# Attention followed by routed experts: blocks behind five groups of the first batch instead of six

## The chip, the cores and the metric

The kernel runs on one core of a Trainium2 chip. The metric is the device time of one execution in microseconds, as the median of several runs. The core's engines are TensorE (matmuls), VectorE, ScalarE, GpSimd (here mostly scatters with indices) and SyncE, which only issues DMAs. Each engine works through its own instructions in the order in which they stand; semaphores make it wait for other engines and for DMAs.

## The reference

Four batches of q, k and v, each 5056 x 256 in float32. Attention is over channels: columns of q and k are normalised over the 5056 tokens, s is a 256 x 256 matrix, and each token's v is multiplied with its softmax. The result goes through a layer of eight experts, of which each token uses the one with the largest logit.

```python
qn = q / (np.linalg.norm(q, axis=1, keepdims=True) + 1e-06)
kn = k / (np.linalg.norm(k, axis=1, keepdims=True) + 1e-06)
s = kn.transpose(0, 2, 1) @ qn / tau
a = softmax(s)                      # over the last axis, 256 x 256
x = (v @ a).reshape(20224, 256)
expert_idx = np.argmax(x @ w_gate, axis=1)
# for each expert e, on its tokens:
h = np.maximum(xe @ w1[e], 0.0)     # 256 -> 1024
out[mask] = gate_w[mask, None] * (h @ w2[e])
```

## The kernel before

For each batch, `attention` first reads q and k in 20 chunks of 256 tokens (`raw`, line 205, 512 KB each). ScalarE squares a chunk (line 217), VectorE adds the squares up (line 218), and TensorE multiplies k with q into two accumulators `sp` (line 225). In the second batch and later a chunk can be split into a high and a low half (`hl`, line 188 on ScalarE, line 189 on VectorE; products in lines 229 and 230). Norms and softmax follow (lines 242 to 303). Then ten groups of 512 tokens each are made into rows of x: TensorE multiplies v with the softmax (`px`, line 365), ScalarE copies the result out and squares it (`xg`, lines 370 and 372), ScalarE and VectorE write two float16 halves of each row (`rows`, lines 386 and 387), VectorE finds the expert, TensorE ranks the tokens of a group within their experts (`rtp`, lines 423 and 426), and GpSimd scatters the rows by expert into `xs` in DRAM, four scatters a group (line 445). The last of the small steps ahead of a group's scatters are the reciprocal in line 433 and the slot numbers in line 442.

`weights` prepares the eight experts' matrices, 16 in all, each loaded in two halves (`W` and `wraw`, line 120). TensorE sums up squares (`gram`, lines 158 and 123), which sets a scale; then ScalarE and VectorE each run once over the matrix to make two float16 halves (lines 112 and 113). It is a generator: each step that is taken from it issues one load.

`table` (lines 500 to 573) turns the counts of the tokens that are scattered so far into a list of full blocks of 256 tokens: `c_tb`, an expert and a place in `xs` for each block (its last step is line 571). `block_load` has SyncE read an entry (line 581), load the block's tokens transposed (`xT`, line 586) and their factors (`mt`, line 588). `block` copies the expert's weights to `wp` (VectorE, line 604), multiplies in two layers (`hp`, line 616, and `y`, line 638), and GpSimd scatters the result to `out` (line 653). There are 72 full blocks and 18 smaller ones. Before a stage's blocks can be loaded, all rows of that stage must be scattered. Stage 0 is made of the first `CUT` groups of the first batch; stage 1 of the whole first batch, and so on.

What is put in which order: the work of the first batch (`first`), the loads of the weights (`wts`) and the first chunks of the second batch (`second`) are interleaved by the loop in line 707, one half of a group of x in each step; a scheduler then orders each engine's instructions. Blocks start behind that loop, and from there the rest of the second batch and all later batches run between the pieces of blocks, paced by the two lists `marks` and `amounts`. `START` makes up for the chunks that were taken already. Buffers set waits too: a chunk of q and k from the second batch on, and a group of v from group `CUT` on, share three buffers (`raw`); `mt` has three, freed by the output scatters of a block.

Of the kernel before, what the change touches and what calls it, by code (L numbers as in the profile page):

```python
# [23 lines left out]
E, F = 8, 1024  # L24
# [3 lines left out]
BLK = 256  # L28
G = 10
T = 4  # L30
CUT = 6

SORTED = [CUT * T * P] + [N * (b + 1) for b in range(B)]
SURE = [-(-(n - E * (BLK - 1)) // BLK) for n in SORTED]
# [29 lines left out]
def attention_then_experts(ctx, tc, qk, vT, wts_in, kc, out):  # L64
# [127 lines left out]
    def attention(b, s_split, x_split, acc):  # L192
# [139 lines left out]
        def v_load(g):  # L332

            if g < CUT and g not in v_ahead:
                v_ahead[g] = [
                    work.tile([P, 512], F32, tag=tag, name=f"v{c}", bufs=bufs)
                    for c, (tag, bufs) in enumerate((("wp", WP), ("ht", 4)))
                ]
                for c in range(2):
                    sync.dma_start(out=v_ahead[g][c], in_=vT[b, g, :, c, :])  # L340

        for g in range(G):
            if b == 0 and g < CUT:
                v_load(g)
# [98 lines left out]
            for t in range(T):  # L443
# [4 lines left out]
                )  # L448
                scattered(0 if b == 0 and g < CUT else b + 1, ins)
            yield 200  # L450
# [6 lines left out]
    def scattered(stage, ins):  # L457
        raw = ins.ins
        for s2 in range(LAST):
            tc.declare_no_dep(raw, group=f"scatter{s2}", reason="slots differ")  # L460
        tc.declare_no_dep(raw, group="loads", reason="blocks read are full already")
        tc.declare_no_dep(raw, group="pads", reason="behind the tokens")
        tc.add_to_no_dep_group(f"scatter{stage}", raw)
        written[stage].append(raw.name)
# [200 lines left out]
    def take(gen, n):  # L665
        for _ in range(n):
            next(gen, None)
        return n

    nch = NP // P // 2  # L670
    normal = [(ps_a, "acc")] * 2
    wts = weights()
# [33 lines left out]
    weighed = 0  # L706
    for step in range(2, nch + 1 + 2 * CUT):
        take(first, 1)
        weighed += take(wts, 0 if step < nch else min(14 if step == nch else 2, 4 * E + 1 - weighed))
        if step > nch + 2:  # L710
            take(second, 1)
    tables = {0: table(0)}
# [13 lines left out]
    ATT = nch * 2 * 640 + 5000 + G * GRP  # L726
    START = -(2 * CUT - 2) * 2 * 640
    marks = [0.0] + [SURE[b] - EARLY for b in range(1, B)]
# [69 lines left out]
```

## Time and profile before

| | |
|---|---|
| median of 3 runs | 1184.86 us (1183.29 to 1185.75) |
| profiled execution | 1188.32 us, span 1186.6 us |
| TensorE busy | 1153.5 us, 97% of the span |
| VectorE busy | 899.4 us, 76% |
| ScalarE busy | 643.5 us, 54% |
| GpSimd busy | 392.3 us, 33% |
| mean granted clock of TensorE | 0.991 |

The time of an execution is a little longer than the span, which runs from the first to the last instruction that the profile shows. The shares are means over the whole span; the first 200 us, where weights are prepared and the first batch is worked through, differ from the rest, where blocks and attention run side by side.

### The profile page before, as it was taken

The numbers are of one execution on the slowest core, as the hardware profiler recorded it, in microseconds if no ns is written. First come the engines' busy times: TensorE is split into PE (matmuls) and PEld (weight loads), VectorE is DVE, ScalarE is ACT, GpSimd is POOL, SyncE is SP. The second block draws the span as 40 slices with busy tenths as digits, with TensorE's granted clock in tenths as the row PEclk, the third lists the DMA queues.
The fourth block names the chain that finished last, engine by engine and source line by source line (L and its number), as shares of the span: only waits on it lengthen the run. The fifth ranks groups of instructions, "written<-read, shape, count | busy, mean of one in ns | idle before, by whom it ended". The sixth has DMA issues, their size and how long they took to land.

```text
span 1186.6 us, 28182 instructions
## 1 busy us (share of the span) xinstructions
PE 1153.5 (97%) x10242; PEld 1024.9 (86%) x10242; DVE 899.4 (76%) x2384; ACT 643.5 (54%) x1362; POOL 392.3 (33%) x366
## 2 busy tenths in 40 slices
PE   9798899999999999999999999999999999999998
PEld 8677688899888889999888889999988888889897
DVE  6789988778887877777888777776875566656886
ACT  6399854877655536665565536666533223332232
POOL 0046761466511123544422212455421111112121
PEclk9989989999999999999999999999999999999999
DMA  9977765445555524444354434443242222111121
GB/s 340 408 277 254 208 177 134 135 122 145 139 145 120 130 81 101 118 115 119 97 152 127 131 91 93 131 95 82 70 109 50 50 55 55 46 51 38 40 52 35
DMA packets 147871, 145.93 MB, mean 123 GB/s; under 512 B 115980, under 2 KB 117393, under 8 KB 147728
## 3 DMA queue, kind: packets, MB, share of 16 engines
q1 hardware_dynamic: 132336, 102.48, 33.0%
q0 software_dynamic: 15392, 41.60, 9.8%
q8 instruction: 82, 1.34, 0.5%
q14 instruction: 61, 0.50, 0.1%
HBM read 80.03 MB, written 43.29 MB: 104 GB/s over the span
## 4 chain that ended last, share of the span: by engine, by line
PE 57%; issue 24%; DVE 7%; POOL 5%; ACT 3%; DMA 3%; SPq 1%; POOLq 0%; DVEq 0%; ACTq 0%
PE y L638 20%; PE hp L616 19%; PE px L368 7%; POOL out L653 4%; PE sp L225 4%; PE sp L229 3%; DMA raw<-in_qk 2%; PE sp L230 2%; DVE W L113 1%; ACT xjunk L372 1%; PE px L365 1%; DVE rows L387 1%; DVE hl L189 1%; ACT W L112 1%; ACT xg L370 1%
## 5 line engine op out<-in xcount | busy, mean ns | idle before, releaser
L616 PE MATMUL hp<-xT,wp 128*128 128x256 f16 (+1 forms) x4320 | 450.0, 262 | 1.6 <-DVE ht L624 1.1
L638 PE MATMUL y<-wp,ht 128*128 128x256 f16 x3888 | 447.7, 273 | 0.0
L616 PEld LDWEIGHTS <-wp 128*128 128x128 f16 x4320 | 383.1, 98 | 46.1 <-issue 3.4
L638 PEld LDWEIGHTS <-ht 128*128 128x128 f16 x3888 | 373.9, 98 | 53.3 <-issue 4.7
L653 POOL DMA_INDIRECT out<-o,mt x162 | 184.9, 1141 | 628.5 <-ACT o L651 595.2
L604 DVE COPY wp<-W 128x1024 f16 x720 | 297.8, 425 | 116.0 <-PE y L638 65.3
L623 ACT ACTIVATE ht<-hp 128x512 f16<-128x512 f32 x324 | 191.6, 593 | 157.1 <-PE hp L616 143.1
L624 DVE SCALAR_TENSOR_TENSOR ht<-hp,ht 128x512 f16<-128x512 f32 x324 | 219.6, 686 | 22.6 <-ACT ht L623 16.6
L445 POOL DMA_INDIRECT xs<-rows,r_si x160 | 189.5, 1184 | 122.7 <-issue 41.8
L651 ACT ACTIVATE o<-y,b_fac 128x256 f32<-128x256 f32 x162 | 68.8, 470 | 207.2 <-PE y L638 196.6
L368 PE MATMUL px<-a_h,hl 128*128 128x264 f32 x480 | 98.1, 296 | 0.0
L386 ACT ACTIVATE rows<-xg,x_sc 128x256 f16<-128x256 f32 x160 | 69.9, 497 | 25.7 <-DVE r_ex L419 16.0
L368 PEld LDWEIGHTS px<-a_h,hl 128*128 128x128 f32 x480 | 78.8, 188 | 1.6 <-issue 0.6
L189 DVE TENSOR_TENSOR hl<-raw,hl 128x1024 fp32r<-128x1024 f32 x47 | 57.4, 1221 | 26.7 <-ACT hl L188 26.7
L188 ACT CAST hl<-raw 128x1024 fp32r<-128x1024 f32 x47 | 49.1, 1044 | 45.2 <-PE sp L230 38.2
L229 PE MATMUL sp<-hl 128*128 128x512 f32 x188 | 72.3, 418 | 1.1 <-DVE hl L189 1.1
L225 PE MATMUL sp<-raw 128*128 128x256 f32 x264 | 65.3, 403 | 7.5 <-DMA raw<-in_qk 7.5
L387 DVE SCALAR_TENSOR_TENSOR rows<-xg,x_sc,rows 128x256 f16<-128x256 f32 x160 | 69.5, 477 | 1.2 <-ACT rows L386 0.8
L217 ACT ACTIVATE raw<-raw 128x1024 f32<-128x1024 f32 x44 | 46.6, 1058 | 42.6 <-DVE hl L189 42.4
L372 ACT ACTIVATE xjunk<-xg 128x256 bf16<-128x256 f32 x160 | 66.7, 417 | 3.2
L368 PE MATMUL px<-a_l,hl 128*128 128x264 f32 x240 | 68.2, 284 | 0.0
L225 PEld LDWEIGHTS sp<-raw 128*128 128x128 f32 x264 | 52.0, 202 | 15.9 <-DMA raw<-in_qk 8.6
(144 smaller groups left out, 926.4 us busy)
## 6 DMA issues: line engine op xcount, KB each, us to landing
raw<-in_qk SPq DMA_DIRECT2D x80, 512.0 KB, 4.2
vraw<-in_vT SPq DMA_DIRECT2D x34, 512.0 KB, 5.1
W<-in_w SPq DMA_DIRECT2D x28, 512.0 KB, 8.5
v<-in_vT SPq DMA_DIRECT2D x12, 256.0 KB
out<-o,mt POOLq DMA_INDIRECT x162, 2.4
xs<-rows,r_si POOLq DMA_INDIRECT x160, 4.0
wraw<-in_w SPq DMA_DIRECT2D x4, 512.0 KB, 6.5
xT<-xs SPq DMA_TRANSPOSE x90, 3.9
```

The source lines that it names most:

```text
L225: pe.matmul(sp[c][:, 0, :], raw[:, j, kc0 : kc0 + P], raw[:, j, 0:C], start=first, stop=last)
L229: pe.matmul(sp[c], hl[:, 0, j, kc0 : kc0 + P], hl[:, :, j, 0:C], start=first, stop=False)
L368: pe.matmul(px, hl[:, vh, c, ts], ah[:, c, :], start=(n == 0), stop=(n == 5))
L372: act.activation(junk, xg[:, t, 0:C], AF.Square, accum_out=ss[:, t : t + 1])
L387: vec.scalar_tensor_tensor(out=r16[:, t, C : 2 * C], in0=x, scalar=sc[:, t : t + 1], in1=r16[:, t, 0:C], op0=ALU.mult, op1=ALU.subtract,)
L445: ins = pool.indirect_dma_start(out=xs[:, :], out_offset=bass.IndirectOffsetOnAxis(ap=si[:n, t : t + 1], axis=0), in_=rows[:n, t, :], in_o ...
L604: copied[0] = vec.tensor_copy(out=t, in_=Wf[:, ds(e * 8192 + n * 1024, 1024)]).ins
L616: pe.matmul(hp[:, f % nf, :], wp[:, dc, wh, (f % 2) * P : (f % 2 + 1) * P], xT[:, 2 * xh + dc, :], start=(n == 0), stop=(n == 5),)
L623: act.activation(ht[:, 0], hp, AF.Relu)
L624: vec.scalar_tensor_tensor(out=ht[:, 1], in0=hp, scalar=0.0, in1=ht[:, 0], op0=ALU.max, op1=ALU.subtract)
L638: pe.matmul(ys[j], hts[f // nf][:, hh, f % nf, j * P : (j + 1) * P], wp[:, f % 2, wh, :], start=(f == 0 and n == 0), stop=(f == 7 and n == 2),
L653: pool.indirect_dma_start(out=out[:, :], out_offset=bass.IndirectOffsetOnAxis(ap=mt.bitcast(I32)[:, j, 1:2], axis=0), in_=o, in_offset=Non ...
```

## The change

`CUT` goes from 6 to 5. Stage 0 has then three blocks instead of five, and stage 1 nine instead of seven; the loop that precedes the blocks has two steps less, so that two chunks fewer of the second batch are taken in it. The loop takes 10 weight loads at its start instead of 14, which puts the first group of x in front of the third expert's weights, then 2 in each of two steps, and 3 instead of 2 in each later step.

```diff
-CUT = 6
+CUT = 5
...
     for step in range(2, nch + 1 + 2 * CUT):
         take(first, 1)
-        weighed += take(wts, 0 if step < nch else min(14 if step == nch else 2, 4 * E + 1 - weighed))
+        weighed += take(wts, 0 if step < nch else min(10 if step == nch else 2 if step < nch + 3 else 3, 4 * E + 1 - weighed))
         if step > nch + 2:
             take(second, 1)
```

On SyncE's queue, behind the 20 chunks of the first batch, loads of weights (`W`) and of v for the first groups stood like this before:

```order
L120 DMA W<-in_w 128x1024 x14
L340 DMA v_518<-in_vT 128x512
L340 DMA v_519<-in_vT 128x512
L340 DMA v_522<-in_vT 128x512
L340 DMA v_523<-in_vT 128x512
L120 DMA W<-in_w 128x1024 x4
L340 DMA v_644<-in_vT 128x512
L340 DMA v_645<-in_vT 128x512
L120 DMA W<-in_w 128x1024 x2
L205 DMA raw<-in_qk 128x1024
```

and stand like this now (other numbers, the same tiles):

```order
L120 DMA W<-in_w 128x1024 x10
L340 DMA v_468<-in_vT 128x512
L340 DMA v_469<-in_vT 128x512
L340 DMA v_472<-in_vT 128x512
L340 DMA v_473<-in_vT 128x512
L120 DMA W<-in_w 128x1024 x4
L340 DMA v_594<-in_vT 128x512
L340 DMA v_595<-in_vT 128x512
L120 DMA W<-in_w 128x1024 x3
L205 DMA raw<-in_qk 128x1024
```

The v of the first two groups moved ahead of four loads of weights, and a third weight load came in front of the second batch's first chunk.

Further on in SyncE's queue, from the third block's load on (`c_tb` is a table entry, `xT` and `mt` are the block's loads, `raw` the second batch's chunks), before:

```order
L581 TENSOR_LOAD c_tb
L586 ISA
L586 DMA_TRANSPOSE xT<-xs 128x4x256
L588 ISA
L588 DMA mt<-xs 128x2x2
L205 DMA raw<-in_qk 128x1024 x4
L581 TENSOR_LOAD c_tb
L586 ISA
L586 DMA_TRANSPOSE xT<-xs 128x4x256
L205 DMA raw<-in_qk 128x1024 x3
L588 ISA
L588 DMA mt<-xs 128x2x2
```

and now, from the load of v for the tenth group on:

```order
L349 DMA vraw<-in_vT 128x1024
L581 TENSOR_LOAD c_tb
L586 ISA
L586 DMA_TRANSPOSE xT<-xs 128x4x256
L588 ISA
L588 DMA mt<-xs 128x2x2
L205 DMA raw<-in_qk 128x1024 x7
L581 TENSOR_LOAD c_tb
L586 ISA
L586 DMA_TRANSPOSE xT<-xs 128x4x256
L588 ISA
L588 DMA mt<-xs 128x2x2
```

The tenth group's v now stands between the second and the third block's load; seven chunks (8 to 14) stand between the third and the fourth block's load, where four (11 to 14) stood, and the three chunks that stood between the fourth block's `xT` and `mt` are behind both.

On TensorE, where the first block begins (`px` is a group of x, `rtp` a rank, `sp_714` and `sp_715` or `sp_673` and `sp_674` the second batch's products, `hp` the block's first layer), before:

```order
L426 MATMUL rtp<-r_ex,ones_80 128x8
L365 MATMUL px<-a_x,vraw 128x264 x5
L616 LDWEIGHTS wp
L616 MATMUL hp<-xT,wp 128x256
```

```order
L426 MATMUL rtp<-r_ex,ones_80 128x8
L365 MATMUL px<-a_x,vraw 128x264 x2
L225 MATMUL sp_673<-raw 128x256
L225 MATMUL sp_674<-raw 128x256
L365 MATMUL px<-a_x,vraw 128x264 x2
L616 LDWEIGHTS wp
L616 MATMUL hp<-xT,wp 128x256
```

In the second piece, which is the order now, half of chunk 8 stands in front of the first block; before, 11 chunks were loaded ahead of the blocks' loads, and the first block began before the next was needed.

## Rows read from the trace of the kernel before

**Rows 1.** The page: the granted clock in 40 equal slices, in tenths.

```profile
PEclk9989989999999999999999999999999999999999
```

**Rows 2.** Windows: start:end, length, busy us of each engine, granted clock, DMA share.

```profile
58.50:62.50 4.00, 4.00 (x11) 3.14 (x12) 3.14 (x4) 3.50 (x4) 0.00 (x0) 0.52 1.03 407
...
80.00:100.00 20.00, 19.75 (x140) 16.77 (x139) 18.24 (x45) 18.49 (x41) 14.48 (x10) 0.93 0.76 260
...
100.00:120.00 20.00, 14.15 (x93) 11.59 (x91) 19.39 (x52) 19.56 (x41) 14.68 (x11) 1.00 0.70 236
...
148.40:153.00 4.60, 4.56 (x13) 3.36 (x14) 2.06 (x9) 2.66 (x4) 3.47 (x5) 0.50 0.71 276
```

**Rows 3.** Timeline of TensorE: start, us, line, count, idle before and its releaser.

```profile
58.04 0.59 PE L123 MATMUL gram<-w_dsum,ones 128*128 128x2 f32 x2 [4.88 <-DVE w_diag L162]
...
58.49 5.70 PE L365 MATMUL px<-a_x,v 128*128 128x264 f32 x16
...
125.04 6.03 PE L365 MATMUL px<-a_x,vraw 128*128 128x264 f32 x26
...
148.44 3.78 PE L225 MATMUL sp<-raw 128*128 128x256 f32 x8 [2.88 <-DMA raw<-in_qk]
...
186.13 1.47 PE L616 MATMUL hp<-xT,wp 128*128 128x256 f16 x12 [1.06 <-DVE ht L624]
```

**Rows 4.** Chain of waits, 120 to 170 us: start, us, what.

```profile
130.68 5.07 DMA xs<-rows,r_si
...
135.90 1.34 SPq L586
...
143.04 5.36 DMA raw<-in_qk
...
152.22 2.49 PE hp L616 x12
...
156.16 1.73 PE sp L225 x8
...
163.55 1.31 PE hp L616 x12
```

**Rows 5.** Timeline of GpSimd, scatters and outputs; columns as in rows 3.

```profile
106.24 1.29 POOL L445 DMA_INDIRECT xs<-rows,r_si  x1 [3.08 <-DVE scales L85]
...
107.84 2.95 POOL L445 DMA_INDIRECT xs<-rows,r_si  x1 [0.30 <-ACT W L112]
...
121.06 3.80 POOL L445 DMA_INDIRECT xs<-rows,r_si  x1 [0.30 <-issue]
...
130.68 0.96 POOL L445 DMA_INDIRECT xs<-rows,r_si  x1 [0.30 <-issue]
...
165.21 2.10 POOL L434 TENSOR_SCALAR rows<-kt 128x4 int32<-128x4 f32 x1
```

**Rows 6.** Timeline of VectorE, same columns.

```profile
105.26 0.17 DVE L433 RECIPROCAL rows<-r_z 128x4 f32<-128x4 f32 x1
...
107.59 2.35 DVE L113 SCALAR_TENSOR_TENSOR W<-W,scales 128x2048 f16<-128x2048 f32 x1
...
109.86 1.67 DVE L387 SCALAR_TENSOR_TENSOR rows<-xg,x_sc,rows 128x256 f16<-128x256 f32 x4
...
115.89 1.23 DVE L218 TENSOR_TENSOR ssq<-ssq,sq 128x1024 f32<-128x1024 f32 x1
...
133.73 0.15 DVE L571 TENSOR_SCALAR c_tb<-c_sf 1x5 int32<-1x5 f32 x1
...
155.06 0.19 DVE L439 TENSOR_TENSOR r_sl<-rtp,r_ex 128x32 f32<-128x32 f32 x1 [4.52 <-PE rtp L426]
```

**Rows 7.** Timeline of ScalarE, same columns.

```profile
50.91 3.90 ACT L112 ACTIVATE W<-W,scales 128x2048 f16<-128x2048 f32 x2 [2.74 <-DVE W L113]
...
158.42 1.04 ACT L188 CAST hl<-raw 128x1024 fp32r<-128x1024 f32 x1 [0.94 <-DVE ssq L218]
```

**Rows 8.** Timeline of SyncE, DMAs issued, same columns.

```profile
174.49 0.39 SPq L588 DMA_DIRECT2D mt<-xs  x1
```

## The prediction

> **What bounds the kernel now.** I read the page first. TensorE is busy 97% of the span (the table above), and the clock row reads 9 except in the third and sixth of its 40 slices [rows 1]. TensorE's instructions are the same before and after but for their order, so a change of time can only come from its idle time and its slow clock, and these sit ahead of 190 us. The windows say why: between 80 and 120 us VectorE is busy 37.6 of 40 us and ScalarE 38.1 [rows 2]. That stretch prepares weights on both (two scalings take 3.90 us on ScalarE, one takes 2.35 on VectorE [rows 6, 7]) and makes the rows of x. The timeline of TensorE shows its holes: 4.88 us ahead of 58.04, 2.88 ahead of 148.44, 1.06 ahead of 186.13 [rows 3]. Behind a long hole the clock is low: 0.52 granted from 58.5 to 62.5 us and 0.50 from 148.4 to 153 [rows 2], the lower level, 1.2 GHz. So the first group of x takes 5.70 us for 16 matmuls where 26 take 6.03 later [rows 3], 2.0 us lost, and behind 148.44 the chunk and the first 12 matmuls of a block lose (3.78 - 1.73) + (2.49 - 1.31) = 3.2 us [rows 3, 4].
>
> The chain of waits then tells what the start of the blocks hangs on: the last scatter of the sixth group (issued 130.68, landed 5.07 later), the load of the first block's xT by SyncE at 135.90, two more of these, and only behind them on the same queue the next 512 KB of q and k, issued at 143.04 and landing 5.36 later, on which TensorE waits until 148.44 [rows 3, 4]. GpSimd's scatters from 106.24 to 131.64 are one queue: twelve, with no gap over 0.4 us [rows 5]. This chain, not the share of busy time, is what the change touches.
>
> **The change part by part.** I count from two marks: T, where SyncE issues the first xT, and R, where TensorE goes on behind the load that follows the three xT.
>
> Scatters. Five groups instead of six: T now waits for the 20th scatter, not the 24th. Before, the fourth group's scatters began at 106.24, behind a row whose reciprocal stood at 105.26, and the 20th began at 121.06 and took 3.80 [rows 5, 6]: 18.6 us for eight. In the new order VectorE has one weight scaling (2.35) and one addition of squares (1.2) less ahead of that reciprocal, so the eight begin 3.5 us earlier, at 102.7. At 18.6 us again they end at 121.3. From the end of the 24th (131.64) to T were 4.3 us [rows 4, 5], so T' is 125.6.
>
> Table. Ahead of the first table VectorE has less to do: one scaling (2.35), two additions (2.4), eight halves of rows (two times 1.67) and about 24 small ones at 0.1, together 10.5 us [rows 6]. Its last step moves from 133.73 to 123.2 and is not the last to come.
>
> First group ahead of the third expert. On TensorE it now stands behind the second expert's sum instead of the third's, which closes the hole at 58.04, so it can start in that hole or before it and at full clock; the 4.88 and the 2.0 of slow clock go. But TensorE is not what comes next: VectorE runs one scaling behind the other there. ScalarE had a hole of 2.74 us there and then waited again [rows 7], and the group's copies can fill that. A lead of the chain of 0 to 4 us is possible (0 if VectorE alone decides, 4 from most of TensorE's 4.88); both engines work in step, and VectorE is full, so I take 1.0. That gives T' = 124.6.
>
> Three weight loads per half group. The same 32 loads in fewer steps; the row of 58.5 to 62.5 us shows the DMA engines full already (share 1.03 [rows 2]), so bytes come no faster. Two chunks of the second batch are taken later: that is 8 matmuls' records each, 1.73 us of TensorE [rows 4], which it must do behind R.
>
> From T' to R'. Before, R is T + 12.54. Now a load of v stands between the second and the third xT, 0.45 us with its gap, where an mt's issue takes 0.39 [rows 8]: R' = 124.6 + 13.0 = 137.6. What TensorE had done before R and still has to do after R': three chunks (5.2), 36 matmuls of the first block at 1.31 per 12 (3.9), four records of a px (0.9), one rank (0.3), 10.3 us. It is where it was at 148.44 by 147.9. The gain is 0.5 us; the slow clock of 3.2 us comes behind R' as it did behind R. The last px of the ninth and tenth group, which ScalarE must copy first, end about then too, so an earlier T' is not worth its full length.
>
> Fewer blocks ahead. Stage 0 has three blocks in place of five, and the fourth block's xT waits for all 40 scatters. On SyncE the chunks 15 and up (counted from 0) stand behind this xT and its mt. TensorE comes to chunk 15 after six chunks (10.4), a split one (1.4), 180 matmuls of blocks (19.7), px and ranks (1.3) and the slow clock (3.2): 137.6 + 36.0 = 173.6. The load needs 5.36, the split 1.04 on ScalarE and about 1.2 on VectorE, as an addition of its size [rows 4, 6, 7], so it must be issued by 166.0. Before, the mt of the fourth block went at 174.49, held by the first block's output scatters, which stood behind the 40 scatters on GpSimd [rows 8]. Now the tenth group's rank on TensorE comes at about 148.7; before, VectorE waited 4.52 us for it until 155.06 [rows 6], so it came near 154.8; behind it VectorE still has an addition and the group's rows to do (2.9), so the last four scatters start 4.6 sooner, and the outputs now stand ahead of a step of GpSimd that was in front of them (2.10 and its gap of 0.27 [rows 5]): the mt goes at 167.5, and a stall of about 1.5 us results. The hole of 1.06 us at 186.13 had the like cause and goes. Net loss 0.4.
>
> **Contention.** A scatter beside a scaling takes 2.95 us, others 0.96 and 1.29 [rows 5, 6]. The Trainium skill (GPSIMD Engine Reference, Key points) says that GpSimd shares its interfaces to SBUF with VectorE and contends with instructions that read two tensors from there; the trace agrees (2.95 us from 107.84, scaling from 107.59). By that rule the denser scalings and one or two more additions beside the eight scatters add some 1.2 us to T', and the sum would be a loss of 1.1 instead of a gain.
>
> Sum: 0.5 - 0.4 = 0.1 us of gain on the profiled execution's 1188.32. That run is 3.46 us above the median 1184.86 of the runs shown, so the forecast is 1184.8, no change that can be told.
>
> Bounds. Best: each of the eight scatters at 1.3 and the full lead; then the table binds, T' = 123.2 - 4 = 119.2, gain 5.9, and with the hole at 186.13 gone 7. Worst: each scatter at 2.95 + 0.3, 26 us, T' = 133, loss 7.9.
>
> **Rivals.**
> 1. The lead holds. ScalarE fills its holes early, both engines come 3 to 4 us sooner to the table and the scatters: gain about 4.5, 1180. For it: ScalarE is as full as VectorE from 80 to 120. Against: VectorE has hardly a hole to give.
> 2. The wait moves to the fourth block. Its place is SyncE's queue in front of chunk 15; it decides from the point where that load goes later than 166.0, and each us later costs one on TensorE. If the outputs of the first block free the mt no sooner than before (174.49), the chunk goes right behind it and the stall is 8.9 us, and at half of it the time is about 1189; full, 1193. For it: the fourth block needs all rows two blocks sooner, and GpSimd's queue holds outputs behind scatters. Against: the tenth group is ranked earlier.
> 3. The change does not act: the start of the blocks is set by weights and by ScalarE's copies of the last groups, since all ten groups' px stand ahead of the first block on TensorE in both orders. Then R' gains what ScalarE gains, 2 us, less the later chunks: 1185.
>
> **How the numbers follow.** About 0.2% (2.4 us) is what can be told from no change. Forecast 0.48, own range 1180.5 to 1188: faster 0.13, same 0.27, slower 0.08. Rival 1, 0.25: faster 0.25. Rival 2, 0.20: slower 0.19, same 0.01. Rival 3, 0.07: faster 0.02, same 0.04, slower 0.01. Together faster 0.40, same 0.32, slower 0.28. The range 1177 to 1190 leaves out the best bound's end and the full stall of rival 2.
>
> **What would show it.** Right: the first xT issued at 124 to 126, held by a scatter; TensorE waiting for a load of q and k at about 137 to 138; its hole at 53 us gone; a hole of 1 to 2 us at about 174 with a split as releaser. Wrong: a T' below 122 or above 129, a hole over 4 us ahead of chunk 15, or TensorE held by ScalarE's copies at the first block.

## The result: slower by 1.1%

The changed kernel took 1199.55 us (median of 4 runs, 1198.93 to 1200.09), the kernel before on the same chip 1185.23 (4 runs): a ratio of 1.0114, interval 1.0093 to 1.0134. The forecast was 1184.8 with a range to 1190; the time lies beyond even the full stall of rival 2 (1193). The profiled execution took 1200.09 us, 11.8 more than the one of before. The count for the third table on TensorE, at 305.75 us before, comes at 317.34; the last one at 853.49 and 864.99. So the whole loss is made ahead of 305 us.

The page of the changed kernel: span, busy time and share by engine, and two rows of its 40 slices. In [rows 1] the third and the sixth slice of the clock were below 9; now it is the second, the third and the seventh.

```profile
span 1198.3 us, 28178 instructions
...
PE 1161.2 (97%) x10242; PEld 1028.5 (86%) x10242; DVE 899.8 (75%) x2384; ACT 643.0 (54%) x1362; POOL 380.5 (32%) x366
...
PE   9878979999999999999999999999999999999998
...
PEclk9889998999999999999999999999999999999999
```

TensorE's timeline answers to [rows 3]: start, duration, instructions, and in brackets the idle time before and what ended it.

```profile
53.16 5.95 PE L365 MATMUL px<-a_x,v 128*128 128x264 f32 x16
...
79.28 0.80 PE L229 MATMUL sp<-hl 128*128 128x512 f32 x1 [4.14 <-DVE hl L189]
...
140.03 1.03 PE L225 MATMUL sp<-raw 128*128 128x256 f32 x4
...
141.78 0.60 PE L616 MATMUL hp<-xT,wp 128*128 128x256 f16 x4
...
170.40 0.48 PE L229 MATMUL sp<-hl 128*128 128x512 f32 x1
...
171.90 2.79 PE L638 MATMUL y<-wp,ht 128*128 128x256 f16 x24
182.05 0.80 PE L229 MATMUL sp<-hl 128*128 128x512 f32 x1 [7.36 <-DVE hl L189]
...
184.78 2.68 PE L638 MATMUL y<-wp,ht 128*128 128x256 f16 x12
187.29 1.47 PE L616 MATMUL hp<-xT,wp 128*128 128x256 f16 x12
```

The hole ahead of 58.04 is gone: the first group runs at 53.16, though no faster (5.95 us against 5.70; the granted clock was 0.62 from 50 to 60 us). The hole ahead of 148.44 is gone too: chunk 8 at 140.03 waits for nothing. In their place stand 4.14 us ahead of the first split chunk and 7.36 us ahead of chunk 15. Behind the second, the eight products of the split chunk take 2.73 us (182.05 to 184.78) where the chunk at 170.40 took 1.50, and 12 matmuls of a block take 2.51 (184.78 to 187.29) where [rows 4] have 1.31: another 2.4 us at the low clock.

The windows of the changed kernel (busy time of PE, PEld, DVE, ACT and POOL with counts, then the clock, DMA share and GB/s) show how complete the standstill is: VectorE does nothing from 170 to 180 us.

```profile
170.00:180.00 10.00, 4.69 (x38) 3.81 (x36) 0.00 (x0) 0.31 (x1) 1.80 (x2) 0.85 0.60 149
180.00:190.00 10.00, 7.95 (x40) 6.26 (x40) 8.78 (x13) 6.57 (x9) 1.46 (x1) 0.64 0.54 154
```

What it waits for is read from the queues. SyncE first (start and duration of an issue), then GpSimd, then the first instruction on ScalarE behind the wait; they answer to [rows 8], [rows 5] and [rows 7]:

```profile
126.99 1.33 SPq L586 DMA_TRANSPOSE xT<-xs  x1
...
134.31 24.20 SPq L205 DMA_DIRECT2D raw<-in_qk  x7
170.83 1.81 SPq L586 DMA_TRANSPOSE xT<-xs  x1
175.39 0.41 SPq L588 DMA_DIRECT2D mt<-xs  x1
175.93 0.87 SPq L205 DMA_DIRECT2D raw<-in_qk  x2
```

```profile
119.15 1.61 POOL L445 DMA_INDIRECT xs<-rows,r_si  x1 [0.30 <-issue]
...
133.41 1.15 POOL L445 DMA_INDIRECT xs<-rows,r_si  x1 [7.50 <-ACT rows L386]
...
160.40 4.62 POOL L445 DMA_INDIRECT xs<-rows,r_si  x1 [0.30 <-ACT sq L217]
...
167.72 1.49 POOL L445 DMA_INDIRECT xs<-rows,r_si  x1 [0.31 <-ACT ht L623]
...
171.13 0.98 POOL L653 DMA_INDIRECT out<-o,mt  x1 [0.31 <-issue]
```

```profile
179.69 1.04 ACT L188 CAST hl<-raw 128x1024 fp32r<-128x1024 f32 x1 [12.09 <-DMA raw<-in_qk]
```

Seven chunks (8 to 14) go out behind the third xT; then SyncE waits for the fourth block's xT until all 40 scatters have landed (170.83), then for its mt until the first block's outputs have left (175.39), and only then issues chunk 15, which lands at 179.67. TensorE's last work ahead of it ended at 174.7.

How much each stretch costs follows from the traces of both kernels on one chip (c2_before, c1_after and c3_behind, below). I count TensorE's records up to a time, each at its distance from the next one at full clock (a chunk's matmul 0.216 us, a block's 0.107, a split chunk's pair 0.35, a px 0.226, later 0.123, the small ones likewise):

| us of work done by | 110 us | 160 us | 190 us | 320 us |
|---|---|---|---|---|
| before | 90.0 | 125.8 | 154.1 | 277.3 |
| changed | 86.2 | 125.0 | 143.9 | 265.0 |
| changed, chunks 15 and 16 first | 86.3 | 126.6 | 151.7 | 272.5 |

Of the loss of 12.3 at 320 us (the spans differ by 12.8), 0.8 is there at 160, 9.4 come from 160 to 190, and 2.1 behind. The 0.8 is about what two executions of one program differ by: on the chip of the result the kernel before had done 125.1 by 160 us, and the changed kernel 125.0. So what the change costs and gains on TensorE ahead of 160 us nearly cancels on these two chips.

### The profile page after: what moved, and what is told of

Its sections match the earlier page's. It is cut to its first block, busy times and chain, and to the rows that moved or that the text cites. A ratio compares the mean times of both kernels' runs of the same rounds, so it can differ in the third digit from the quotient of the medians.

```text
span 1198.3 us, 28178 instructions
## 1 busy us (share of the span) xinstructions
PE 1161.2 (97%) x10242; PEld 1028.5 (86%) x10242; DVE 899.8 (75%) x2384; ACT 643.0 (54%) x1362; POOL 380.5 (32%) x366
## 4 chain that ended last, share of the span: by engine, by line
PE 51%; issue 24%; POOL 5%; DVE 5%; ACT 2%; DMA 1%; POOLq 0%; DVEq 0%; SPq 0%; ACTq 0%
PE y L638 19%; PE hp L616 19%; PE px L368 7%; POOL out L653 5%; PE sp L229 3%; PE sp L230 2%; DVE ht L624 1%; DVE hl L189 1%; DVE rows L387 1%; DVE wp L604 1%; ACT xjunk L372 1%; ACT xg L370 0%; POOL xs L445 0%; DMA out<-o,mt 0%; ACT hl L188 0%
## 5 line engine op out<-in xcount | busy, mean ns | idle before, releaser
L653 POOL DMA_INDIRECT out<-o,mt x162 | 181.3, 1119 | 634.9 <-ACT o L651 601.5
L445 POOL DMA_INDIRECT xs<-rows,r_si x160 | 184.4, 1153 | 140.3 <-issue 43.5
L386 ACT ACTIVATE rows<-xg,x_sc 128x256 f16<-128x256 f32 x160 | 70.0, 498 | 29.6 <-DVE r_ex L419 16.2
L229 PE MATMUL sp<-hl 128*128 128x512 f32 x188 | 74.3, 428 | 11.5 <-DVE hl L189 11.5
L370 ACT COPY xg<-px 128x264 f32<-128x264 f32 x160 | 57.4, 365 | 11.7 <-PE px L368 8.7
```

The costliest lines, as they stand in the source:

```text
L229: pe.matmul(sp[c], hl[:, 0, j, kc0 : kc0 + P], hl[:, :, j, 0:C], start=first, stop=False)
L386: act.activation(r16[:, t, 0:C], x, AF.Copy, scale=sc[:, t : t + 1])
L445: ins = pool.indirect_dma_start(out=xs[:, :], out_offset=bass.IndirectOffsetOnAxis(ap=si[:n, t : t + 1], axis=0), in_=rows[:n, t, :], in_o ...
L653: pool.indirect_dma_start(out=out[:, :], out_offset=bass.IndirectOffsetOnAxis(ap=mt.bitcast(I32)[:, j, 1:2], axis=0), in_=o, in_offset=Non ...
```

## The experiments

The kernel before took 1186 us on the chip of c1_after, c2_before and c3_behind, about as on that of the result, but about 1218 on the other four. So each ratio is to the runs of before on the same chip, and traces are compared only between chips of the same kind. In the expectations, theory Q is that the fourth block's loads ahead of chunk 15 on SyncE cost the time, and theory W that the third weight load does, through VectorE; rival P is that another wait or an earlier stretch does, and rival L that the changed order of the weights' loads does.

**The fourth block's loads behind chunks 15 and 16.** The order of the instructions on all other engines stays.

```diff
+        with tc.issue_after(last_load[1]) if (stage, i) == (1, 0) else nullcontext():
             at = nc.values_load(...)
...
-        look(n + 1)
+        look(n + (n != 2))
...
-            if k == 0:
-                look(n + 2)
+            if k == (2 if n == 2 else 0) and n != 1:
+                look(n + 1); look(n + 2)
```

c1_after, the changed kernel: 

> The changed kernel once more, beside the next two on one chip, since on the chip of the first four experiments the kernel before took 1219 us in place of 1185, 34 us more than the edits could move. Theory Q (TensorE starves at chunk 15 behind the fourth block's loads): ratio to before 1.008 to 1.013, hole of 6 to 8 us near 175 us. Rival C (the loss of 1.1% was one of that chip and that day): ratio 0.998 to 1.005.

c2_before: 

> The kernel before, one profile, so that every experiment of this call has a trace of before from the same chip beside it. Theory Q: hole of under 2 us ahead of the split chunk at 186 us. If the chip is one like that of the first four experiments, 1213 to 1225 us with more idle time of VectorE and ScalarE between 140 and 160 us; if one like the first, 1183 to 1188.

c3_behind: 

> The changed kernel with the fourth block's xT and mt behind chunks 15 and 16 on SyncE's queue, again, now beside the changed kernel on one chip. Theory Q: 6 to 11 us faster than the changed kernel, its hole near 175 us gone; ratio to before 0.999 to 1.004. Rival P (another wait takes its place): less than 3 us faster than the changed kernel.

On a chip with 1186.13 us for the kernel before, the changed kernel took 1199.14 (1197.95 to 1200.27; ratio 1.0098, 1.0064 to 1.0132), and with the two chunks ahead 1194.58 (1192.46 to 1197.31; 1.0075, 1.0054 to 1.0097). The profiled spans are 1185.7 (before), 1198.5 and 1191.0. SyncE, the holes of TensorE, and two windows of this kernel:

```profile
132.52 34.18 SPq L205 DMA_DIRECT2D raw<-in_qk  x9
170.37 1.27 SPq L586 DMA_TRANSPOSE xT<-xs  x1
174.35 0.41 SPq L588 DMA_DIRECT2D mt<-xs  x1
175.25 1.25 SPq L586 DMA_TRANSPOSE xT<-xs  x1
176.55 1.52 SPq L205 DMA_DIRECT2D raw<-in_qk  x3
```

```profile
183.50 0.50 PE L229 MATMUL sp<-hl 128*128 128x512 f32 x1 [2.80 <-DVE hl L189]
...
186.51 1.49 PE L616 MATMUL hp<-xT,wp 128*128 128x256 f16 x12 [1.33 <-DVE ht L624]
```

```profile
170.00:180.00 10.00, 10.00 (x84) 8.68 (x83) 4.19 (x6) 2.11 (x2) 1.28 (x2) 1.00 0.55 126
180.00:190.00 10.00, 5.87 (x44) 4.74 (x42) 7.32 (x10) 7.63 (x11) 2.42 (x2) 1.00 0.48 162
```

The wait moves with the queue: chunks 15 and 16 are in time, chunk 17 behind the two xT is late by 2.80 us. The clock stays at 1.00 (2.4 GHz). By the median 4.6 us come back (7.5 between the profiled spans), less than the 6 to 11 expected, and the ratio is above the expected 0.999 to 1.004: theory Q holds for the place and the mechanism, but does not give the whole loss. By the table 3.2 us are still lost from 160 to 190, at these two holes, against the kernel before, and 2.4 behind, whose cause no run shows. Rival C falls: the loss is there on a second chip.

**The same on another chip, and six mt buffers.** The second kernel has `bufs=6` for mt:

```diff
-        mt = work.tile([P, 2, 2], F32, tag="mt", name="mt", bufs=3)[...]
+        mt = work.tile([P, 2, 2], F32, tag="mt", name="mt", bufs=6)[...]
```

e5_behind: 

> The changed kernel with the fourth block's xT and mt behind chunks 15 and 16 on SyncE's queue in place of ahead of them; nothing else is moved on any engine. Theory Q: the hole at 174 to 182 us goes to under 1.5 us and the clock stays at 2.4 GHz there; 1187 to 1191, the 10 us that TensorE lost from 170 to 190 us come back, and the 2 us that the changed kernel was ahead at 160 us may show as a gain over before. Rival P: the wait comes back one place further on, 1195 to 1200. Rival L: 1195 to 1200.

e3_mt6: 

> The changed kernel with six buffers for mt in place of three, so that the fourth block's mt no longer waits for the output scatters of the first block; its xT still waits for all 40 scatters of rows (170.8 us). Theory Q: SyncE gets to chunk 15 at 171 to 172 in place of 175.9, the hole of 7.4 us shrinks to 3 to 4, and with it part of the slow clock: 1193 to 1197. Rival P: 1198 to 1200, the same as changed. Rival L: 1198 to 1200.

Before took 1219.34 us here. e5_behind: 1231.32, ratio 1.0102 (1.0061 to 1.0142); e3_mt6: 1227.75, 1.0063 (1.0039 to 1.0088). The times decide nothing on chunk 15, since on this chip TensorE has no idle time over 1 us between 165 and 195 us in either: it is held up ahead of 160 us (last section) and comes late to chunk 15. What e3_mt6 shows is how the two waits add up. SyncE:

```profile
170.10 1.25 SPq L586 DMA_TRANSPOSE xT<-xs  x1
171.57 0.41 SPq L588 DMA_DIRECT2D mt<-xs  x1
172.65 0.33 SPq L205 DMA_DIRECT2D raw<-in_qk  x1
```

The mt goes 1.5 us behind its xT, against 4.1 in e1_cut_only (below) on the same chip and 4.6 in the changed kernel; chunk 15 goes 2.6 us behind the xT, against 4.7 and 5.1. So 2 to 3 us of SyncE's wait are the output scatters, and the wait ahead of the xT is the scatters of rows. The edit also brings three mt of later blocks in front of chunk 16.

**One chunk more.** In the changed kernel three chunks ahead of the fourth block's loads, one more ahead of the fifth's.

```diff
-            if k == (2 if n == 2 else 0) and n != 1:
-                look(n + 1); look(n + 2)
+            if k == (4 if n == 2 else 0) and n != 1:
+                look(n + 1); look(n + 2 - (n == 2))
```

f1_behind3: 

> The changed kernel with chunks 15, 16 and 17 ahead of the fourth block's xT and mt on SyncE's queue, and one more chunk ahead of the fifth block's xT; nothing else is moved. With two chunks ahead the hole went from 7.7 to 2.8 and 1.3 us and stood at chunk 17. Theory Q: with three it goes at chunk 17 too, 2 to 5 us faster than with two, ratio to before 1.001 to 1.006. Rival P (the rest of the loss is made earlier): within 1.5 us of the run with two, ratio 1.006 to 1.009, though the hole is smaller.

i3_behind3: 

> The changed kernel with chunks 15, 16 and 17 ahead of the fourth block's loads and one more ahead of the fifth's. Theory Q: no hole over 1.5 us between 165 and 195 us; 2 to 4 us faster than with two chunks ahead (ratio 1.0075), ratio to before 1.003 to 1.006, what is left being theory W's. Rival P (the rest is all made ahead of 150 us): 1.006 to 1.009.

k3_behind3: 

> The changed kernel with three chunks ahead of the fourth block's loads. On a chip where the kernel before takes some 1186 us: theory Q no hole over 1.5 us between 165 and 195 us and a ratio of 1.003 to 1.006; the rival (the rest is made ahead of 150 us) 1.006 to 1.009. On a chip with some 1218 us: 1.007 to 1.010 as so far.

All three ran on chips with 1218 us: 1228.52 (ratio 1.0081, 1.0058 to 1.0104), 1229.93 (1.0092, 1.0056 to 1.0128), 1232.13 (1.0128, 1.0101 to 1.0155), the first two slower than theory Q expected, the last above the 1.007 to 1.010 expected for such a chip. No hole over 1.5 us at 165 to 195 us, but there is none with CUT = 5 alone on such chips either. Inconclusive: whether the rest at chunk 17 would go on a chip with 1186 isn't known.

**The two lines of the change by themselves.**

```diff
+CUT = 5        (e1, g1, i1, k1: this alone)
...
+        weighed += take(wts, ... min(10 if step == nch else 2 if step < nch + 3 else 3, ...))
                (e2, g2, i2, k2: this alone, CUT = 6)
```

e1_cut_only: 

> CUT = 5 alone, with the weights' loads of before (14 at the loop's start, then 2). Theory Q (the fourth block's loads stand on SyncE ahead of chunk 15 and wait for scatters, TensorE starves there and then runs at the low clock): still slower than before by 7 to 12 us, 1192 to 1197, with a hole over 4 us in TensorE at 170 to 185 us whose last releaser is a half of a chunk, chunk 15 or 16, loaded behind the fourth block's mt. Rival L (the other order of the weights' loads and of the first group of x is what costs, through the clock of 0.74 at 40 to 60 us and the hole at 79 us): within 3 us of before, 1182 to 1188. Rival P (the pace of ScalarE and VectorE ahead of 150 us costs, the hole only takes the place of another wait): 1190 to 1199, no word on the hole.

g1_cut_only: 

> CUT = 5 alone, with the weights' loads of before, again, since the first run of it was on a chip where the kernel before took 34 us more. Theory Q: hole over 4 us at chunk 15 or 16, ratio to before 1.005 to 1.011. Rival L (the changed order of the weights' loads costs): ratio under 1.003.

i1_cut_only: 

> CUT = 5 with the weights' loads of before. Theory Q (the fourth block's loads stand ahead of chunk 15 or 16 on SyncE): a hole over 4 us there, ratio to before 1.004 to 1.009. Theory W (the third weight load a half group puts a second scaling ahead of the split of chunk 0 on VectorE; TensorE waits 4.1 us at 79 us and then runs slow): this hole is under 1.5 us here. Rival: CUT = 5 costs nothing by itself, ratio under 1.003.

k1_cut_only: 

> CUT = 5 alone. On a chip where the kernel before takes some 1186 us: theory Q a hole of 4 us or more at chunk 15 or 16 behind the fourth block's loads and a ratio to before of 1.004 to 1.010; the rival (CUT = 5 costs nothing without the other loads' order) a hole under 2 us and a ratio under 1.003. On a chip with some 1218 us: no such hole, ratio 1.006 to 1.010 as in the three runs so far.

e2_loads_only: 

> CUT = 6 as before, with the changed weights' loads alone (10, then 2, 2, then 3). Theory Q: no hole at chunk 15 beyond the 1 us of before; within 3 us of before, 1182 to 1188, and rather below, since the product of busy time and clock of the changed kernel was 2 to 3 us ahead of before at 60 to 70 us. Rival L: slower by 5 to 12 us, 1190 to 1197. Rival P: 1185 to 1190.

g2_loads_only: 

> CUT = 6 with the changed weights' loads alone, again. Theory Q: ratio to before 0.997 to 1.002. Rival L: ratio over 1.004; TensorE's work is then 3 us or more behind the kernel before at 110 to 120 us, as in the changed kernel.

i2_loads_only: 

> CUT = 6 with the changed weights' loads (10, 2, 2, then 3). Theory W: the hole at 77 to 80 us is 3 to 4.5 us long, nothing over 2 us at the fourth block, ratio to before 1.002 to 1.006. Rival Q alone: ratio 0.998 to 1.002, the hole at 79 us being paid by the one at 58 us that goes.

k2_loads_only: 

> The changed weights' loads alone. On a chip where the kernel before takes some 1186 us: theory W a hole of 4.1 us at 78 us and a ratio of 1.001 to 1.005; the rival (the gain at 58 us pays for it) 0.997 to 1.001. On a chip with some 1218 us: 1.003 to 1.006 as so far.

All eight ran on chips with 1218 us. Ratios (intervals): CUT alone 1.0069 (1.0045 to 1.0092), 1.0086 (1.0060 to 1.0111), 1.0088 (1.0063 to 1.0113), 1.0090 (1.0059 to 1.0120); loads alone 1.0053 (1.0025 to 1.0081), 1.0034 (1.0009 to 1.0058), 1.0053 (1.0031 to 1.0075), 1.0086 (1.0055 to 1.0118). No interval holds 1: each line costs by itself there, CUT = 5 some 8 to 11 us, the loads 4 to 10. So rival L was right that the loads cost (g2's 1.0034 lies just under its 1.004, k2's 1.0086 above the 1.003 to 1.006 expected) and wrong that CUT = 5 alone costs nothing, and Q alone doesn't explain the whole. The hole at chunk 15 is in none of them: what either line costs on these chips has another cause, and it stays open. The changed kernel with both lines and nothing else was not run there.

**The third weight load.** CUT = 6 and the first group early, but two loads a half group; and, for both lines, CUT = 5 with the loads of before and the three chunks ahead.

```diff
-... min(14 if step == nch else 2, 4 * E + 1 - weighed))
+... min(10 if step == nch else 2, 4 * E + 1 - weighed))
```

j1_first_only: 

> CUT = 6, the first group of x in front of the third expert's weights as in the change, but two loads a half group as before. Theory W: one scaling ahead of the split of chunk 0 as before, the hole at 79 us under 1.5 us and the one at 58 us gone: ratio to before 0.996 to 1.001. Rival V (VectorE and ScalarE are full from 60 to 120 us, so what TensorE gains at 58 us it waits for later in any order): 0.999 to 1.002 with another hole of 2 us or more between 60 and 120 us. Rival F (the earlier first group itself costs): over 1.003.

h1_cut_behind3: 

> CUT = 5 with the weights' loads of before, and the order of SyncE's queue of the first kernel of this call (three chunks ahead of the fourth block's loads). Theories Q and L both: the best of the four if both edits cost; ratio to before 0.998 to 1.003. If the order of the weights' loads gained: 1 to 4 us slower than the first kernel of this call.

j1: 1223.26 us, ratio 1.0044 (1.0016 to 1.0073), beside i2's 1.0053 on the same chip. TensorE's wait for the first split chunk, of i2 and then of j1; then VectorE ahead of it, of i2 and of j1:

```profile
77.70 0.79 PE L229 MATMUL sp<-hl 128*128 128x512 f32 x1 [4.14 <-DVE hl L189]
```

```profile
70.85 0.50 PE L229 MATMUL sp<-hl 128*128 128x512 f32 x1 [1.15 <-DVE hl L189]
```

```profile
71.90 4.61 DVE L113 SCALAR_TENSOR_TENSOR W<-W,scales 128x2048 f16<-128x2048 f32 x2
76.43 1.22 DVE L189 TENSOR_TENSOR hl<-raw,hl 128x1024 fp32r<-128x1024 f32 x1
```

```profile
66.49 2.35 DVE L113 SCALAR_TENSOR_TENSOR W<-W,scales 128x2048 f16<-128x2048 f32 x1
...
69.58 1.22 DVE L189 TENSOR_TENSOR hl<-raw,hl 128x1024 fp32r<-128x1024 f32 x1
```

The hole is the third load's: two scalings ahead of the split in place of one. It is 4.1 us long in every kernel with the changed line, 1.15 in those without it, on chips of both kinds. But taking it away didn't take away the loss: the intervals of i2 and j1 overlap, and theory W, as an account of the time, isn't borne out; by its number, rival F fits (over 1.003). h1: 1227.94, 1.0079 (1.0052 to 1.0107), above the 0.998 to 1.003 expected and no gain over f1's 1.0081 on its chip. No version ran faster than the kernel before.

## Why the prediction was wrong

**The step that failed: "Fewer blocks ahead".** It said: the last four scatters start 4.6 us sooner, "the mt goes at 167.5, and a stall of about 1.5 us results". The mt went at 175.39, 0.9 later than before [rows 8]; the stall was 7.36, and 2.4 of low clock stood behind it, for which neither the sum nor the rivals had a term. This is rival 2, which had a chance of 0.20, in nearly its full size (8.9): TensorE came 1.1 us later than reckoned, chunk 15 went about 1 us later than the rival had it, and it landed in 3.74 us instead of 5.36. TensorE's arrival was forecast at 173.6 and was 174.7; the forecast of the issue was what failed. That the arrival came so near is in part luck: the first block began later than reckoned, and the 3.2 us of slow clock that were counted on the way did not come.

Why it failed can be read on four engines. The slot numbers of the tenth group did come 5 us sooner (151.26 against 156.30), as reckoned, but GpSimd was behind. ScalarE around the rows of the sixth group, now and then before:

```profile
120.92 1.99 ACT L112 ACTIVATE W<-W,scales 128x2048 f16<-128x2048 f32 x1
...
126.07 1.99 ACT L112 ACTIVATE W<-wraw,scales 128x2048 f16<-128x2048 f32 x1
127.97 1.69 ACT L386 ACTIVATE rows<-xg,x_sc 128x256 f16<-128x256 f32 x4
```

```profile
115.46 1.69 ACT L386 ACTIVATE rows<-xg,x_sc 128x256 f16<-128x256 f32 x4
...
118.24 1.99 ACT L112 ACTIVATE W<-W,scales 128x2048 f16<-128x2048 f32 x1
...
122.92 2.00 ACT L112 ACTIVATE W<-wraw,scales 128x2048 f16<-128x2048 f32 x1 [1.75 <-DVE W L113]
```

The last two scalings, which stood behind the sixth group's rows, now stand ahead of them: 16 where 14 stood. (Ahead of the fourth group's rows there are 10 in place of 11, as reckoned, but ahead of the fifth's 14 in place of 13.) They are some 4 us on ScalarE, and its rows came 12.5 us later. The rest is ahead of ScalarE: with `CUT` = 5 the sixth group is no longer one of the loop's, and its v is no longer a tile of its own but shares the three `raw` buffers with the chunks. SyncE and TensorE, before and then now:

```profile
92.81 0.98 SPq L340 DMA_DIRECT2D v<-in_vT  x2
...
103.70 1.94 PE L365 MATMUL px<-a_x,v 128*128 128x264 f32 x8
```

```profile
115.03 9.79 SPq L349 DMA_DIRECT2D vraw<-in_vT  x4
...
118.98 9.93 PE L365 MATMUL px<-a_x,vraw 128*128 128x264 f32 x36 [0.38 <-DMA vraw<-in_vT]
```

Its v went out 22 us later and its products began 15 us later; they waited last for this load, though only 0.38 us. Which of the delays would have bound without the others was not tried. Its scatters began at 133.41 in place of 125.22, and [rows 5] show its last one at 130.68; GpSimd had idled 7.50 us. From there its queue didn't catch up, one scatter took 4.62 us, and the last ended at 169.2 in place of 165.1. The step of GpSimd that the prediction put behind the outputs still stood ahead of them, but took 0.22 us (at 169.28) in place of 2.10. I had followed the moved work up to the first mark, T, but not through to the 40th scatter, which the change needs two blocks sooner.

**T'** was 126.99 against 124.6, and 135.90 before. The 20th scatter ended at 120.76, close to the forecast of 121.3, and it was not a scatter that held T', as I had said, but the table: its last step stood at 125.92 (forecast 123.2), with a scaling in the middle of its steps on VectorE.

```profile
123.48 2.35 DVE L113 SCALAR_TENSOR_TENSOR W<-W,scales 128x2048 f16<-128x2048 f32 x1
...
125.92 0.16 DVE L571 TENSOR_SCALAR c_tb<-c_sf 1x3 int32<-1x3 f32 x1
```

The eight scatters of the fourth and fifth group took 11.3 us of their own time (11.5 in c1_after), where they had taken 16.2; but they took 12.3 in c2_before, so most of this differs between two executions of one program. The 1.2 us more that I had worked out by the Trainium skill (GPSIMD Engine Reference, Key points) did not come, though a long one (2.52 at 105.54) again lay beside a scaling.

**R'** does not exist. TensorE was 3.8 us of work behind the kernel before at 110 us, and the products of the sixth and later groups stood ahead of its first block until 141.78; chunk 8 was there when it came. T' came 8.9 us earlier, but the first block began 2.3 us later than before (139.49): what earlier blocks were to gain was gone, much as in rival 3. The sign that I had named, TensorE held by ScalarE's copies, is there only with 0.48 us (ahead of 130.49).

**The lead** of the first group was taken as 1.0. TensorE was 3.8 us of work ahead at 70 us and 0.6 behind at 80: VectorE decided, as the lower bound said. The 2.0 us of slow clock in the first group stayed. And the third load, which I had costed at nothing ("bytes come no faster"), put a second scaling in front of the split. The cost was on VectorE, not in the bytes.

**The holes.** The prediction's list left out the second longest ahead of 190 us, in which TensorE waited for a chunk. In the changed kernel the longest hole there is 2.16 (ahead of 110.94); the sum had no term for it.

```profile
119.99 0.90 PE L225 MATMUL sp<-raw 128*128 128x256 f32 x2 [4.31 <-DMA raw<-in_qk]
```

Right were that the hole ahead of the first group goes and that a split ends the last hole. T' lies between the 124 to 126 named as right and the 129 named as wrong.

**Open**: the 2.1 us behind 190, what held the sixth group above all, and how the 13 us divide between the two lines on a chip with 1186 us. On chips with 1218 both lines cost.

## What to carry to other kernels

When an edit makes a stage start sooner, find what the next stage needs in full, and follow the moved work through to that point on every engine: work that is taken from the front of a mark stands behind it, ahead of the next one, and a load that loses a buffer of its own waits behind others. On a queue that works in order, a load that waits for data holds every load behind it, also those that are free to go; ask which engine needs the third and fourth entry behind the wait. And a load that costs no bytes can still cost its consumer's place in another engine's order.

## What the runs showed of the hardware

The chip mattered more than the change. The same program took 1194.58 us on the chip of c3_behind and 1231.32 on that of e5_behind; the kernel before 1186 and 1218. In e5_behind ScalarE and VectorE stop together from 146.6 us on, and TensorE behind them from 148.7 (the timeline of all engines):

```profile
149.86 0.60 ACT L623 ACTIVATE ht<-hp 128x512 f16<-128x512 f32 x1 [3.22 <-remote]
149.87 0.47 DVE L604 COPY wp<-W 128x1024 f16 x1 [3.25 <-remote]
...
153.39 0.21 PE L423 MATMUL rtp<-r_ex,tri 128*128 128x32 f16 x1 [4.71 <-DVE ht L624]
```

ScalarE and VectorE wait there for no instruction that the profile names, only `remote`. TensorE idles 4.7 to 8.8 us between 140 and 162 us in all fifteen runs on the chips with 1218 us, and 1.2 to 2.6 in the three runs on the chip with 1186. The cause wasn't tried, the kernel before was not profiled on a chip with 1218 us, and the stops are too short to be the whole 32 us. Where such stops lie, a hole of another kind can't show itself, and an experiment that should take it away shows nothing.

The length of a hole alone did not tell whether the clock fell behind it. With holes of 2.80 and 1.33 us it stayed at 1.00 from 180 to 190 us (c3_behind), with one of 7.36 it was 0.64 (changed kernel), which cost 2.4 us. But behind 2.88 us in the kernel before it was 0.50 [rows 2], and behind 2.56 us at the same place in c2_before 0.62 (149 to 153.5 us).
